# Two attention decodes on one core: the second half of every value chunk is copied to the spare buffer, and the last ten chunks load their keys in pieces

## The chip, the core and the metric

The kernel runs on one core of a Trainium2 chip. The metric is the time of one launch on the device in microseconds (us); the median of several launches counts. The core has a matmul engine (PE), a vector engine (DVE), a scalar engine (ACT), a general engine (POOL, called Pool below) and a sequencer that here only issues transfers (SP). Sixteen DMA engines carry the transfers between the memory of the chip (DRAM) and the core's on-chip buffer.

## The reference: what is computed

There are two independent decode steps of attention (one new token for each of four sequences); their results stand side by side in the output. For each, with `x` of 4 x 512, 32 query heads of width 128, and bf16 data:

```python
q = x @ wq                                   # 4 x 32 heads x 128
scores = einsum("bhqd,bhkd->bhqk", q, k) * 128 ** -0.5
p = softmax(scores)
o = einsum("bhqk,bhkd->bhqd", p, v)
out = o.reshape(4, 4096) @ wo                # 4 x 512
```

Problem A has 8 key heads, each shared by four query heads, and uses only the last 2048 positions of its cache. Problem B has 32 key heads and all 8192 positions: its keys and values are 4 x 32 x 8192 x 128 each, 268 MB of keys and as many of values, and each number is used once. Nearly all of the 587 MB that the kernel reads is this.

## The kernel before, in words

**Chunks.** Problem A is done first, in 8 chunks. Problem B follows in 32 chunks, which I number b0 to b31; the code's number is 8 more (`NCA` is 8, `NC` is 40, so `NC - 1` is b31 and `NC - 10` is b22). A B chunk is one sequence and four heads: 256 tiles of 128 positions x 128 for the keys (8.39 MB) and 256 tiles for the values (8.39 MB).

**Buffers.** `kv` has ten units; each holds 64 tiles. Units 0 to 3 (`KB`) take a B chunk's keys, units 4 to 7 (`VB`) its values, units 8 and 9 (`KX`) are the spare buffer. PE reads the first half of the keys in `KB`, and the second half in `KX`. For most chunks the keys come in one DMA into units 0 to 3, and Pool then copies the second half to `KX` in four copies of 32 tiles (L396), so that units 2 and 3 come free early. b0 and b27 to b31 are different: their keys come in pieces, and the pieces of the second half go straight to `KX`, with no copy. The values come in one DMA (in pieces for b27 to b31) and are read where they land.

**What a B chunk does (`whole_B`).** PE transposes each key tile into PSUM (L448, the groups "tr"), eight to a group; DVE (L517) or ACT (L515) copies a group to the buffer `kt`; PE multiplies it with the query (L450, "sc"). The 32 groups of a chunk run in order, with the score of a group two groups behind its transpose. Then come the maximum, the exponentials (ACT, L635), the sums (DVE, L640), with a reordering of the output weights beside them (PE L450 "tr<-wos", DVE L751). Then PE multiplies all 256 value tiles (L450, "po<-pbb,kv"), and the result is normalized (L725); its product with the output weights ("fin") is done in the next chunk. PE does all this in one fixed order, with no work of another chunk in between.

**What orders the transfers.** All of them are issued by SP from one list in program order: K(b0), V(b0), K(b1), V(b1) and so on, with the output weights `wos` behind the keys of every fourth chunk. SP stands still at an issue until the buffer is free, and all that follows on the list stands behind it. The list `held` says what frees a unit. A whole K(n+1) waits for the transposes of the first half of chunk n (units 0 and 1) and for the copies of the second half (units 2 and 3). V(n+1) waits for the last product of chunk n's values (key `("pv", c)`), for all four units (L412, issue at L415). The copies into `KX` wait for the transposes of the chunk before.

**How PE hears of a landing.** Pool stands between: for each landing it raises a counter (`relay`, a wait and an increment), `r_k` for the first half of the keys, `r_c` for the second (there the copy itself raises it), `r_v` for the values. Pool, too, works through one list in order. PE waits for steps of these counters: `QK` and `QC` for groups of key tiles, `QV` for the values.

Of the kernel before, what the change touches and what calls it, by code (L numbers as in the profile page):

```python
# [11 lines left out]
I32 = mybir.dt.int32  # L12

P = 128
TG = 8
NTRB = 3
NKT = 4
NH = 10
# [2 lines left out]
NSM = 2  # L21
SLAG = 2
NW = 64
LASTK = (32, 32, 64, 64, 64)
HALVES = (128, 128)
NEXTK = (64, 64, 64, 64)
NEXTV = (128, 64, 32, 32)
LASTV = (128, 64, 32, 16, 8, 8)
QK = (0, 4, 8)
QC = (16, 20, 24, 28)  # L30
QV = (0, 16, 24, 28, 30, 31)

TRM0, BC0, L0, Q0, XT0 = 0, 256, 288, 320, 448
Z0 = Q0
# [137 lines left out]
def bass_concat_heads__sliding_block_cached__mha_block_cached__decode_kernel(  # L172
# [23 lines left out]
    chunks = []  # L196
# [5 lines left out]
    NC = len(chunks)  # L202
    NCA = Hkv
# [8 lines left out]
    NTA, NTB = chunks[0]["NT"], chunks[-1]["NT"]  # L212
    NONE = NC
    chunks.append(dict(chunks[NCA]))
    assert sum(LASTV) == sum(LASTK) == sum(NEXTK) == sum(NEXTV) == NTB and NTA * 16 == 1024 and NTB * 4 == 1024

    sch = _Sched()
    with ExitStack() as es:
        block = es.enter_context(nc.Block())

        def sb(name, shape, dt):
            return es.enter_context(nc.sbuf_tensor(name, shape, dt))

        def ps(name, shape, dt):
# [4 lines left out]
        wos = sb("wos", [P, 4, DO], BF16)  # L229
# [36 lines left out]
        fin = ps("fin", [P, 512], F32)  # L266
        xtps = ms[:, XT0:XT0 + KC * NB].bitcast(BF16)

        semnames = ["eng_pe", "eng_dve", "eng_act", "eng_pool", "eng_sp", "d_x0", "d_x1", "d_o0", "d_o1", "r_k", "r_v"]
        semnames += ["d_h%d" % i for i in range(NH)] + ["d_bk0", "d_bv0", "r_c"]  # L270
        semnames += [f + str(i) for f, x in (("d_lk", LASTK), ("d_nk", NEXTK), ("d_fk", HALVES), ("d_lv", LASTV), ("d_nv", NEXTV), ("d_hv", HALVES)) for i in range(len(x))]
        semnames += ["d_wo%d" % i for i in range(NWO)] + ["d_wos"]
        sems = {n: es.enter_context(nc.semaphore(n)) for n in semnames}
# [15 lines left out]
            waits=["c_onesf", "c_identf"], key="c_ind")  # L289
# [26 lines left out]
        half_of = {}  # L316
        held = [[] for _ in range(NH)]
# [10 lines left out]
        def flat(at, n):  # L328
            return kv[:, at:at + n, :].rearrange("p s x -> p (s x)")
# [21 lines left out]
        def dma_wos(hq):  # L351


            src = B_wo[4 * hq * P:4 * (hq + 1) * P, :].rearrange("(p r) n -> p (r n)", r=4)
            sch.add_dma("sp", lambda e: e.dma_start(wos[:, :, :].rearrange("p r n -> p (r n)"), src), "d_wos",
                        waits=[("reord", NCA + 4 * hq - 1)] if hq else [], key=("wos", hq))

        def dma_A(kind, c):
# [4 lines left out]
            src = T[:, ch["g"], SkA - W:, :].rearrange("b (pp j) d -> pp b (j d)", pp=P // NB)  # L363
            sch.add_dma("sp", lambda e: e.dma_start(kv[:, at, :], src), "d_h%d" % at, waits=waits, key=(kind, c))

        def dma_K(c):


            ch, i0, half = chunks[c], c - NCA, NTB // 2
            src = B_k[ch["b"], 4 * ch["hq"]:4 * ch["hq"] + 4].rearrange("u (pp j) d -> (u pp) (j d)", pp=P // 4)  # L370
            T = [("T", ch["s"] + (u + 1) * NTB // 4 // TG - 1) for u in range(4)]
            wos = [("wos", ch["hq"])] if ch["b"] == 0 else []
            if c in PIECES_K:
                fam, pieces = PIECES_K[c]
                j0 = 0
                for i, n in enumerate(pieces):
                    at = KB if j0 < half else KX
                    dst = flat(at, 2)[:, (j0 % half) * P:(j0 % half + n) * P]
                    waits = []
                    for u in range(j0 % half * 4 // NTB, (j0 % half + n - 1) * 4 // NTB + 1):  # L380
                        waits += held[at + u]
                    x = slice(j0 * P, (j0 + n) * P)
                    sch.add_dma("sp", lambda e, x=x, dst=dst: e.dma_start(dst, src[:, x]), fam + str(i), waits=waits, key=("k", c, i))
                    j0 += n
                    if wos and j0 == NTB:
                        dma_wos(ch["hq"])
                    sch.relay("pool", sems, "r_k" if j0 <= half else "r_c", n // TG, [("k", c, i)] + (wos if j0 == NTB else []))
            else:
                sch.add_dma("sp", lambda e: e.dma_start(flat(KB, 4), src), "d_bk0", waits=held[KB] + held[KB + 1] + held[KB + 2] + held[KB + 3], key=("k", c, 0))
                if wos:  # L390
                    dma_wos(ch["hq"])
                sch.relay("pool", sems, "r_k", half // TG, [("k", c, 0)])
                for k in range(4):
                    x = slice(k * half // 4 * P, (k + 1) * half // 4 * P)
                    sch.ops["pool"].append((
                        lambda e, x=x: e.tensor_copy(flat(KX, 2)[:, x].bitcast(I32), flat(KB + 2, 2)[:, x].bitcast(I32)),  # L396
                        tuple(held[KX + k // 2] + [("k", c, 0)] + (wos if k == 3 else [])), ("r_c", half // 4 // TG), None))
                held[KB + 2] = held[KB + 3] = [("cp", c)]
                sch.tk[("cp", c)] = ("r_c", (i0 + 1) * half // TG)
            held[KB], held[KB + 1], held[KX], held[KX + 1] = [T[0]], [T[1]], [T[2]], [T[3]]  # L400
            for steps, name in ((QK, "r_k"), (QC, "r_c")):
                for g, end in zip(steps, steps[1:] + (steps[0] + half // TG,)):
                    sch.tk[("kr", c, g)] = (name, i0 * half // TG + end - steps[0])

        def dma_V(c):

            ch = chunks[c]
            src = B_v[ch["b"], 4 * ch["hq"]:4 * ch["hq"] + 4].rearrange("u (pp j) d -> (u pp) (j d)", pp=P // 4)
            dst = flat(VB, 4)
            fam, pieces = PIECES_V.get(c, ("d_bv", (NTB,)))  # L410
            j0 = 0
            waits = held[VB] + held[VB + 1] + held[VB + 2] + held[VB + 3]  # L412
            for i, n in enumerate(pieces):
                x = slice(j0 * P, (j0 + n) * P)
                sch.add_dma("sp", lambda e, x=x: e.dma_start(dst[:, x], src[:, x]), fam + str(i), waits=waits, key=("v", c, i))  # L415
                j0 += n
                sch.relay("pool", sems, "r_v", n // TG, [("v", c, i)])
            for g, end in zip(QV, QV[1:] + (NTB // TG,)):
                sch.tk[("vr", c, g)] = ("r_v", (c - NCA) * (NTB // TG) + end)
            for u in range(4):  # L420
                held[VB + u] = [("pv", c)]

        KB, VB, KX = 0, 4, 8
        PIECES_K = {NCA: ("d_fk", HALVES), NC - 5: ("d_fk", HALVES), NC - 4: ("d_fk", HALVES),
                    NC - 3: ("d_nk", NEXTK), NC - 2: ("d_nk", NEXTK), NC - 1: ("d_lk", LASTK)}
        PIECES_V = {NC - 5: ("d_hv", HALVES), NC - 4: ("d_hv", HALVES), NC - 3: ("d_nv", NEXTV), NC - 2: ("d_nv", NEXTV), NC - 1: ("d_lv", LASTV)}

        dma_x(0)
        dma_x(1)
# [16 lines left out]
        def pe_mm(o, l, r, start=True, stop=True, transpose=False, waits=(), key=None):  # L446
            if transpose:
                sch.add("pe", lambda e: e.transpose(o, l, r), waits, key)  # L448
            else:
                sch.add("pe", lambda e: e.matmul(o, l, r, start=start, stop=stop), waits, key)  # L450
# [35 lines left out]


        def tile_of(kind, c, j):
            if c >= NCA and kind == "k":
                return flat(KB if j < NTB // 2 else KX, 2)[:, j % (NTB // 2) * P:(j % (NTB // 2) + 1) * P]  # L490
            at = half_of[(kind, c)] if c < NCA else VB
            return flat(at, chunks[c]["NT"] // NTA)[:, j * P:(j + 1) * P]

        bank_used = [None] * NTRB

# [181 lines left out]
        def emit_pv(c, g):  # L677
            ch = chunks[c]
            UC = ch["UC"]
            base = 16 * (c % NSM) if ch["ab"] == 0 else 0  # L680
            for t in range(TG):
                j = g * TG + t
                n = NW
                waits = [("exp", c) if c < NCA else ("exp", c, 0)] + po_read if j == 0 else []
                if j == 0:
                    po_read[:] = []
                for k in (1, 2):
                    if c >= NCA and j == EXPS[k][0] - NW // 4:
                        waits = [("exp", c, k)]
                if c >= NCA:  # L690
                    waits += [("vr", c, g)] if t == 0 and g in QV else []
                elif j == 0:
                    waits += [("v", c)]
                pe_mm(po[:, base:base + n], tile_of("v", c, j), pbt[ch["ab"]][:, par(c), j * UC:j * UC + n],
                      start=j == 0, stop=j == ch["NT"] - 1, waits=waits, key=("pv", c) if j == ch["NT"] - 1 else None)

        def norm_sum(c):
            if c < NCA:
# [254 lines left out]
```

## Time and profile before

| what | value |
|---|---|
| median of three runs | 1381.54 us (1378.66 to 1383.99) |
| the profiled execution, its own time | 1391.14 us |
| its span, first to last instruction | 1389.4 us |
| busy PE, DVE, ACT, POOL | 90%, 54%, 39%, 15% of the span |
| read from DRAM | 587.21 MB, 423 GB/s over the span |
| granted PE clock, mean | 0.966 |
| one copy of keys by Pool (L396), 104 of them | 1.898 us |
| one copy of transposed keys, DVE (L517) / ACT (L515) | 0.691 us / 1.024 us |

The profile is of one execution, whose own time is 9.6 us above the median of the runs without a profile. [...] "DMA to landing" is the time from the issue of a transfer to its completion, and includes waiting behind the transfers before it.

### The profile page before, as it was taken

What the parts mean: (1) busy time and instruction counts of PE and PEld (TensorE: products, weight loads), DVE (VectorE), ACT (ScalarE), POOL (GpSimd) and SP (SyncE); (2) the same over time, 40 slices, a digit from 0 to 9 for tenths busy, and PEclk for the clock granted to TensorE, in tenths of its full rate; (3) what the DMA queues carried; (4) which work ended last, traced back from release to release, by engine and by line L of the source; (5) the groups of instructions that cost most, each with busy time, mean ns of one, the idle gap of its engine ahead of it and who ended that gap; (6) DMA issues with size and microseconds to landing.
All of it is one profiled execution on the core that took longest, in us unless ns stands there. A gap on an engine that the chain in (4) does not pass through costs nothing.

```text
span 1389.4 us, 61669 instructions
## 1 busy us (share of the span) xinstructions
PE 1244.8 (90%) x27673; PEld 1116.6 (80%) x27673; DVE 747.0 (54%) x1335; ACT 547.3 (39%) x777; POOL 202.5 (15%) x133
## 2 busy tenths in 40 slices
PE   4897898989899898989999899898998989999998
PEld 4776787878789787878888888787888878888887
DVE  1675364645455554545555555455655545556555
ACT  1553342434344333434444334343442433444443
POOL 2000022222101222220122222210222222000000
PEclk9998799999999999999999999999999999999999
DMA  9999899999999999999999999999999999999998
GB/s 399 426 425 443 382 423 423 419 425 426 434 394 451 411 419 425 392 438 423 426 449 419 423 441 413 432 438 423 434 411 453 432 428 419 423 428 428 427 428 360
DMA packets 17917, 587.52 MB, mean 423 GB/s; under 512 B 2004, under 2 KB 2024, under 8 KB 4456
## 3 DMA queue, kind: packets, MB, share of 16 engines
q1 hardware_dynamic: 17864, 587.21, 98.7%
q8 instruction: 15, 0.25, 0.1%
q14 instruction: 6, 0.05, 0.0%
q10 hardware_dynamic: 32, 0.01, 0.0%
HBM read 587.21 MB, written 0.01 MB: 423 GB/s over the span
## 4 chain that ended last, share of the span: by engine, by line
DMA 56%; PE 41%; DVE 1%; issue 1%; SPq 0%; POOLq 0%; DVEq 0%
DMA kv<-in_B_k_cache_dram 52%; PE tr L448 22%; PE sc L450 10%; PE po L450 5%; DMA kv<-in_A_k_cache_dram 2%; DMA kv<-in_B_wq_dram 2%; PE fin L450 2%; PE tr L450 1%; PE ms L450 1%; DVE kt L517 0%; DVE wor L751 0%; DVE sA L570 0%; DVE gm L601 0%; PE ms L448 0%; DVE rm L582 0%
## 5 line engine op out<-in xcount | busy, mean ns | idle before, releaser
L448 PE MATMUL tr<-identb,kv 128*128 128x128 bf16 x8704 | 679.9, 223 | 93.6 <-POOLq L75 85.0
L517 DVE COPY kt<-tr 128x1024 bf16<-128x1024 bf16 x736 | 502.7, 691 | 321.5 <-PE tr L448 318.7
L515 ACT ACTIVATE kt<-tr 128x1024 bf16<-128x1024 bf16 x352 | 359.6, 1024 | 693.9 <-PE tr L448 693.7
L448 PEld LDWEIGHTS tr<-identb,kv 128*128 128x128 bf16 x8704 | 520.2, 100 | 108.9 <-issue 87.1
L450 PE MATMUL sc<-qq,kt 128*128 128x64 bf16 x8192 | 402.0, 192 | 13.8 <-DVE kt L517 10.4
L450 PEld LDWEIGHTS sc<-qq,kt 128*128 128x128 bf16 x8192 | 335.7, 99 | 17.5 <-DVE kt L517 13.1
L396 POOL COPY kv<-kv 128x2048 int32<-128x2048 int32 x104 | 192.7, 1898 | 972.0 <-DMA kv<-in_B_k_cache_dram 972.0
L450 PEld LDWEIGHTS po<-pbb,kv 128*128 128x128 bf16 x8192 | 252.1, 99 | 10.7 <-issue 3.0
L450 PE MATMUL po<-pbb,kv 128*128 128x64 bf16 x8192 | 253.7, 194 | 2.4 <-issue 2.4
L635 ACT ACTIVATE pbb<-sc,negb 32x64 bf16<-32x64 f32 (+1 forms) x384 | 171.1, 445 | 131.5 <-DVE negb L615 126.3
L640 DVE TENSOR_REDUCE rsb<-pbb 128x4 f32<-128x1024 bf16 x32 | 39.1, 1220 | 99.8 <-ACT pbb L635 99.8
L751 DVE CAST wor<-tr 128x512 bf16<-128x512 f32 x128 | 80.1, 684 | 1.2 <-PE tr L450 1.2
L450 PE MATMUL po<-sel,identb 128*128 128x512 bf16 x256 | 77.2, 390 | 0.0
L450 PE MATMUL tr<-wos,back 32*128 32x512 bf16 x512 | 68.6, 384 | 3.1
L450 PEld LDWEIGHTS po<-sel,identb 128*128 128x128 bf16 x256 | 19.9, 98 | 39.6 <-issue 28.8
L586 DVE TENSOR_REDUCE rh<-sc 128x4 f32<-128x512 f32 x64 | 43.9, 686 | 14.3 <-PE sc L450 14.3
L450 PEld LDWEIGHTS tr<-wos,back 32*128 32x128 bf16 x512 | 21.7, 94 | 34.5 <-DVE wor L751 19.2
L725 DVE TENSOR_TENSOR oz<-po,rz 128x16 bf16<-128x16 f32 x32 | 5.6, 175 | 70.1 <-PE po L450 70.1
L450 PE MATMUL sc<-qb,kt 128*128 128x64 bf16 (+3 forms) x512 | 26.0, 196 | 0.7 <-DVE gx L607 0.6
L450 PE MATMUL fin<-wor,oz 128*4 128x256 bf16 x264 | 25.1, 324 | 0.4 <-DVE oz L725 0.4
L703 DVE RECIPROCAL rinv<-ms 128x4 f32<-128x4 f32 (+1 forms) x40 | 7.8, 196 | 30.6 <-PE ms L450 30.6
L450 PEld LDWEIGHTS sc<-qb,kt 128*128 128x128 bf16 x512 | 21.6, 101 | 2.7 <-DVE gx L607 1.1
(66 smaller groups left out, 252.2 us busy)
## 6 DMA issues: line engine op xcount, KB each, us to landing
kv<-in_B_v_cache_dram SPq DMA_DIRECT2D x7, 4096.0 KB, 23.1
kv<-in_B_k_cache_dram SPq DMA_DIRECT2D x6, 4096.0 KB, 21.6
kv<-in_B_k_cache_dram SPq DMA_DIRECT2D x11, 2048.0 KB, 30.4
kv<-in_A_k_cache_dram SPq DMA_DIRECT2D x8, 2048.0 KB, 14.6
kv<-in_A_v_cache_dram SPq DMA_DIRECT2D x8, 2048.0 KB, 16.1
kv<-in_B_v_cache_dram SPq DMA_DIRECT2D x3, 2048.0 KB, 30.4
kv<-in_B_v_cache_dram SPq DMA_DIRECT2D x5, 1024.0 KB, 32.4
kv<-in_A_wq_dram SPq DMA_DIRECT2D x1, 4096.0 KB, 12.5
```

The lines of the kernel that those rows point to most:

```text
L396: lambda e, x=x: e.tensor_copy(flat(KX, 2)[:, x].bitcast(I32), flat(KB + 2, 2)[:, x].bitcast(I32)),
L448: sch.add("pe", lambda e: e.transpose(o, l, r), waits, key)
L450: sch.add("pe", lambda e: e.matmul(o, l, r, start=start, stop=stop), waits, key)
L515: sch.add("act", lambda e: e.activation(dst, src, ACTF.Copy), waits=waits, key=("ev", s))
L517: sch.add("dve", lambda e: e.tensor_copy(dst, src), waits=waits, key=("ev", s))
L586: sch.add("dve", lambda e: e.tensor_reduce(out=rh[:, half, :], in_=src, axis=AX.X, op=ALU.max), waits=[("S", ch["s"] + (half + 1) * ch["NG ...
L635: sch.add("act", lambda e, src=src, dst=dst, pp=pp, u=u: e.activation(dst, src, ACTF.Exp, bias=negb[pp, 0, u:u + 1], scale=scale), waits=[ ...
L640: sch.add("dve", lambda e: e.tensor_reduce(out=rst[1][:, :], in_=probs_of(c).rearrange("p j u -> p u j"), axis=AX.X, op=ALU.add), waits=[( ...
L703: sch.add("dve", lambda e: e.reciprocal(out=ri, in_=ms[:, L0:L0 + n]), waits=[("L", c)], key=("rinv", c))
L725: sch.add("dve", lambda e: e.tensor_tensor(out=o, in0=i0, in1=i1, op=ALU.mult), waits=waits, key=("oT", c))
L751: sch.add("dve", lambda e: e.tensor_copy(wol[:, u, :], o), waits=[("reord", c) if u == 3 else ("reord", c, u)] + [("fin", prev(c))], key=( ...
```

## The change

Five things change.

1. Pool copies the second half of the values (units 6 and 7) to `KX` too, with the same four copies, as soon as the values have landed and the chunk's transposes have left `KX`. PE reads that half of the values from `KX`. A new counter `r_w` tells it so. This is done for b0 to b30.
2. V(n+1) now waits for the product of the first half of chunk n's values (units 4 and 5; a new signal in the middle of the product) and for the copies of the second half (units 6 and 7). `KX` now comes free for the keys of chunk n+1 with the product: three quarters of it for unit 8, all of it for unit 9.
3. The keys of b22 to b26 come in halves and those of b27 to b30 in quarters (before: b27 and b28 in halves, b29 and b30 in quarters, the others of these whole). Their second half lands in units 2 and 3 and is copied by Pool, and so is that of b31, whose second half now comes in four pieces in place of two. Only b0's keys still go straight to `KX`.
4. The values of b27 come whole (before: in halves). Those of b28 to b31 keep their pieces.
5. The second half of b31's values lands straight in `KX`, and waits for the transposes of b31's third and fourth quarter.

```diff
-LASTK = (32, 32, 64, 64, 64)
+LASTK = (32, 32, 64, 32, 32, 32, 32)
-QV = (0, 16, 24, 28, 30, 31)
+QV = (16, 20, 24, 28, 30, 31)
...
+        def spread_copies(name, units, waits, first, n, landed, last=()):
+            for k in range(first // 32, (first + n) // 32):
+                x = slice(k * 32 * P, (k + 1) * 32 * P)
+                sch.ops["pool"].append((
+                    lambda e, x=x: e.tensor_copy(flat(KX, 2)[:, x].bitcast(I32), flat(units, 2)[:, x].bitcast(I32)),
+                    tuple(waits[k // 2] + landed + (list(last) if k == 3 else [])), (name, 32 // TG), None))
...
 dma_K:
+            direct = c == NCA
+            units = [KB, KB + 1] + ([KX, KX + 1] if direct else [KB + 2, KB + 3])
...
+                    if direct:
+                        sch.relay("pool", sems, "r_c", (j0 + n - half - first) // TG, [key] + end)
+                    else:
+                        spread_copies("r_c", KB + 2, [held[KX], held[KX + 1]], first, j0 + n - half - first, [key], end)
...
 dma_V:
-            waits = held[VB] + held[VB + 1] + held[VB + 2] + held[VB + 3]
+            direct = c == NC - 1
+            units = [VB, VB + 1] + ([KX, KX + 1] if direct else [VB + 2, VB + 3])
...
+                    else:
+                        spread_copies("r_w", VB + 2, [held[KX], held[KX + 1]], first, j0 + n - half - first, [key])
...
-            for u in range(4):
-                held[VB + u] = [("pv", c)]
+            if not direct:
+                held[VB + 2] = held[VB + 3] = [("cw", c)]
+                sch.tk[("cw", c)] = ("r_w", (i0 + 1) * half // TG)
+            held[VB] = held[VB + 1] = [("pv", c, 2)]
+            held[KX], held[KX + 1] = [("pv", c, 3)], [("pv", c)]
...
-        PIECES_K = {NCA: ("d_fk", HALVES), NC - 5: ("d_fk", HALVES), NC - 4: ("d_fk", HALVES),
-                    NC - 3: ("d_nk", NEXTK), NC - 2: ("d_nk", NEXTK), NC - 1: ("d_lk", LASTK)}
-        PIECES_V = {NC - 5: ("d_hv", HALVES), NC - 4: ("d_hv", HALVES), NC - 3: ("d_nv", NEXTV), NC - 2: ("d_nv", NEXTV), NC - 1: ("d_lv", LASTV)}
+        PIECES_K = {NCA: ("d_fk", HALVES), NC - 1: ("d_lk", LASTK)}
+        PIECES_K.update({c: ("d_fk", HALVES) for c in range(NC - 10, NC - 5)})
+        PIECES_K.update({c: ("d_nk", NEXTK) for c in range(NC - 5, NC - 1)})
+        PIECES_V = {NC - 4: ("d_hv", HALVES), NC - 3: ("d_nv", NEXTV), NC - 2: ("d_nv", NEXTV), NC - 1: ("d_lv", LASTV)}
...
 emit_pv (c is the chunk, j its value tile, NTB is 256):
-                      start=j == 0, stop=j == ch["NT"] - 1, waits=waits, key=("pv", c) if j == ch["NT"] - 1 else None)
+                      start=j == 0, stop=j == ch["NT"] - 1, waits=waits,
+                      key=("pv", c) if j == ch["NT"] - 1 else ("pv", c, (j + 1) // 64) if c >= NCA and j in (NTB // 2 - 1, NTB // 4 * 3 - 1) else None)
```

PE, DVE and ACT do the same work in the same order as before; only PE's waits and signals around the value products differ. Pool has 248 copies in place of 104, and SP has a few more issues.

More of the change, by code (lines that the diff above doesn't have):

```diff
@@ L267, in bass_concat_heads__sliding_block_cached__mha_block_cached__decode_kernel @@
         xtps = ms[:, XT0:XT0 + KC * NB].bitcast(BF16)
-        semnames = ["eng_pe", "eng_dve", "eng_act", "eng_pool", "eng_sp", "d_x0", "d_x1", "d_o0", "d_o1", "r_k", "r_v"]
+        semnames = ["eng_pe", "eng_dve", "eng_act", "eng_pool", "eng_sp", "d_x0", "d_x1", "d_o0", "d_o1", "r_k", "r_v", "r_w"]
         semnames += ["d_h%d" % i for i in range(NH)] + ["d_bk0", "d_bv0", "r_c"]
@@ L372, in dma_K @@
             wos = [("wos", ch["hq"])] if ch["b"] == 0 else []
[L373 to L397, printed above, removed]
@@ new lines, in dma_K @@
+            direct = c == NCA
+            fam, pieces = PIECES_K.get(c, ("d_bk", (NTB,)))
+            units = [KB, KB + 1] + ([KX, KX + 1] if direct else [KB + 2, KB + 3])
+            landed, j0 = [], 0
+            for i, n in enumerate(pieces):
+                at = units[j0 // 64]
+                waits = []
+                for u in range(j0 // 64, (j0 + n - 1) // 64 + 1):
+                    waits += held[units[u]]
+                x, y = slice(j0 * P, (j0 + n) * P), slice(j0 % 64 * P, (j0 % 64 + n) * P)
+                sch.add_dma("sp", lambda e, x=x, y=y, at=at: e.dma_start(flat(at, NH - at)[:, y], src[:, x]), fam + str(i), waits=waits, key=("k", c, i))
+                landed.append((j0, n, ("k", c, i)))
+                j0 += n
@@ new lines, in dma_K @@
+            if wos:
+                dma_wos(ch["hq"])
+            for j0, n, key in landed:
+                end = wos if j0 + n == NTB else []
+                if j0 < half:
+                    sch.relay("pool", sems, "r_k", min(n, half - j0) // TG, [key])
+                if j0 + n > half:
+                    first = max(j0, half) - half
+                    if direct:
+                        sch.relay("pool", sems, "r_c", (j0 + n - half - first) // TG, [key] + end)
+                    else:
+                        spread_copies("r_c", KB + 2, [held[KX], held[KX + 1]], first, j0 + n - half - first, [key], end)
@@ L405, in dma_V @@
         def dma_V(c):
-            ch = chunks[c]
+            ch, i0, half = chunks[c], c - NCA, NTB // 2
             src = B_v[ch["b"], 4 * ch["hq"]:4 * ch["hq"] + 4].rearrange("u (pp j) d -> (u pp) (j d)", pp=P // 4)
-            dst = flat(VB, 4)
             fam, pieces = PIECES_V.get(c, ("d_bv", (NTB,)))
+            direct = c == NC - 1
+            units = [VB, VB + 1] + ([KX, KX + 1] if direct else [VB + 2, VB + 3])
             j0 = 0
-            waits = held[VB] + held[VB + 1] + held[VB + 2] + held[VB + 3]
@@ L413, in dma_V @@
             for i, n in enumerate(pieces):
-                x = slice(j0 * P, (j0 + n) * P)
-                sch.add_dma("sp", lambda e, x=x: e.dma_start(dst[:, x], src[:, x]), fam + str(i), waits=waits, key=("v", c, i))
-                j0 += n
-                sch.relay("pool", sems, "r_v", n // TG, [("v", c, i)])
+                at = units[j0 // 64]
+                waits = []
+                for u in range(j0 // 64, (j0 + n - 1) // 64 + 1):
+                    waits += held[units[u]]
+                x, y = slice(j0 * P, (j0 + n) * P), slice(j0 % 64 * P, (j0 % 64 + n) * P)
@@ new lines, in dma_V @@
+                sch.add_dma("sp", lambda e, x=x, y=y, at=at: e.dma_start(flat(at, NH - at)[:, y], src[:, x]), fam + str(i), waits=waits, key=("v", c, i))
+                key = ("v", c, i)
+                if j0 < half:
+                    sch.relay("pool", sems, "r_v", min(n, half - j0) // TG, [key])
+                if j0 + n > half:
+                    first = max(j0, half) - half
+                    if direct:
+                        sch.relay("pool", sems, "r_w", (j0 + n - half - first) // TG, [key])
+                    else:
+                        spread_copies("r_w", VB + 2, [held[KX], held[KX + 1]], first, j0 + n - half - first, [key])
@@ L418, in dma_V @@
+                j0 += n
+            if not direct:
+                held[VB + 2] = held[VB + 3] = [("cw", c)]
+                sch.tk[("cw", c)] = ("r_w", (i0 + 1) * half // TG)
+            held[VB] = held[VB + 1] = [("pv", c, 2)]
+            held[KX], held[KX + 1] = [("pv", c, 3)], [("pv", c)]
+            sch.tk[("vr", c, 0)] = ("r_v", (i0 + 1) * half // TG)
             for g, end in zip(QV, QV[1:] + (NTB // TG,)):
-                sch.tk[("vr", c, g)] = ("r_v", (c - NCA) * (NTB // TG) + end)
@@ L420, in dma_V @@
-            for u in range(4):
-                held[VB + u] = [("pv", c)]
+                sch.tk[("vr", c, g)] = ("r_w", i0 * half // TG + end - QV[0])
         KB, VB, KX = 0, 4, 8
-        PIECES_K = {NCA: ("d_fk", HALVES), NC - 5: ("d_fk", HALVES), NC - 4: ("d_fk", HALVES),
-                    NC - 3: ("d_nk", NEXTK), NC - 2: ("d_nk", NEXTK), NC - 1: ("d_lk", LASTK)}
-        PIECES_V = {NC - 5: ("d_hv", HALVES), NC - 4: ("d_hv", HALVES), NC - 3: ("d_nv", NEXTV), NC - 2: ("d_nv", NEXTV), NC - 1: ("d_lv", LASTV)}
+        PIECES_K = {NCA: ("d_fk", HALVES), NC - 1: ("d_lk", LASTK)}
@@ L488, in tile_of @@
         def tile_of(kind, c, j):
[L489 to L492, printed above, removed]
+            if c >= NCA:
+                return flat(KX if j >= NTB // 2 else KB if kind == "k" else VB, 2)[:, j % (NTB // 2) * P:(j % (NTB // 2) + 1) * P]
+            return flat(half_of[(kind, c)], 1)[:, j * P:(j + 1) * P]
         bank_used = [None] * NTRB
@@ L690, in emit_pv @@
                 if c >= NCA:
-                    waits += [("vr", c, g)] if t == 0 and g in QV else []
+                    waits += [("vr", c, g)] if t == 0 and (g == 0 or g in QV) else []
                 elif j == 0:
```

## The prediction

> **What bounds the kernel now.** I read the page first.
>
> ```profile
> PE 1244.8 (90%) x27673; PEld 1116.6 (80%) x27673; DVE 747.0 (54%) x1335; ACT 547.3 (39%) x777; POOL 202.5 (15%) x133
> q1 hardware_dynamic: 17864, 587.21, 98.7%
> DMA kv<-in_B_k_cache_dram 52%; PE tr L448 22%; PE sc L450 10%; PE po L450 5%; DMA kv<-in_A_k_cache_dram 2%; DMA kv<-in_B_wq_dram 2%; PE fin L450 2%; PE tr L450 1%; PE ms L450 1%; DVE kt L517 0%; DVE wor L751 0%; DVE sA L570 0%; DVE gm L601 0%; PE ms L448 0%; DVE rm L582 0%
> ```
>
> PE at 90% and the transfers at 98.7% both look full; the chain of waits says that it is mostly the keys' transfer that ends a wait. So the second view is the chain in order of time, in the steady part:
>
> ```profile
> 984.69 25.98 DMA kv<-in_B_k_cache_dram
> 1010.84 1.06 PE tr L448 x16
> ...
> 1021.87 28.58 DMA kv<-in_B_k_cache_dram
> 1050.62 1.37 PE tr L448 x16
> ...
> 1063.17 26.02 DMA kv<-in_B_k_cache_dram
> 1089.36 1.06 PE tr L448 x16
> ```
>
> Start plus length is the landing of a chunk's keys: 1010.67, 1050.45, 1089.19. PE starts 0.17 us after each, so PE waits for every chunk. The spacings are 39.78 and 38.74, and 38.72 is the shortest that I find (two transfers of 19.36). Why is one longer by 1.04? The third view, SP's issues:
>
> ```profile
> 1009.22 0.33 SPq L415 DMA_DIRECT2D kv<-in_B_v_cache_dram  x1
> 1021.87 0.33 SPq L389 DMA_DIRECT2D kv<-in_B_k_cache_dram  x1
> 1046.39 0.33 SPq L415 DMA_DIRECT2D kv<-in_B_v_cache_dram  x1
> ```
>
> The values of b22 were issued at 1009.22, 1.4 us before the keys ahead of them in the queue had landed; those of b23 at 1046.39, 4.1 us before. Only the first cost time. Over all chunks a lead of 3 us or more costs nothing, 2.15 us (issue at 333.29, keys landed 335.44) costs 1.7, and a negative lead up to 3.4. The view by stretches shows the queue running dry there (last columns: DMA share and GB/s; before them, Pool's busy time and the clock):
>
> ```profile
> 250.00:260.00 10.00, 9.09 (x236) 8.44 (x233) 5.37 (x9) 1.66 (x2) 5.52 (x4) 1.00 0.79 315
> 570.00:580.00 10.00, 9.09 (x250) 8.58 (x247) 4.08 (x9) 1.71 (x3) 3.69 (x3) 1.00 0.77 308
> 1090.00:1100.00 10.00, 10.00 (x229) 9.63 (x227) 6.78 (x10) 4.38 (x5) 6.83 (x4) 1.00 0.98 426
> ```
>
> What holds V back is in SP's waits:
>
> ```profile
> SPq L415 <- PE po L450: 623.1, 32, 40.2
> ```
>
> V(n+1) waits for the last value product of chunk n, which ends 35.5 us after the keys of n landed (1010.84 to 1046.39), or 37.1 where PE had idled before and its clock was granted at 0.83 for a while (1050.62 to 1087.69). The queue ahead of it is empty at 38.7. The lead of 1.6 to 3.2 us is too short.
>
> **What the gaps are worth.** Keys of b1 landed at 173.5 (issue 133.8 and 39.7 to landing), those of b26 at 1168.5: 995.0 us for 25 spacings. At 38.72 they are 968.0; six loads of `wos` lie between, 1.27 each: 7.6. The excess is 19.4 us. V(b26) was late too (issue 1166.42, 1.0 lost): 20.4. Of this, 1.4 stands at chunks whose V was in time; I leave it, and 19.0 remains.
>
> **The change part by part.**
>
> V's wait: the second half of the product takes 3.95 us (256 tiles in 7.9), so the first half ends at 31.6 (slow chunks 33.1) after the keys' landing. The other condition, Pool's copies of V's second half: V lands at 19.4; units 8 and 9 are free after the third and fourth quarter of the transposes, at 16.3 and 21.8 (slow 17.8 and 23.3); a set of four copies takes 7.4 us. Two copies are done by 23.1, two more by 27.0. So V(n+1) is issued at 31.6 to 33.1, a lead of 5.6 to 7.1 us in place of 1.6 to 3.2; every lead over 3 was free. Gain 19.0. At b1, where most is lost (V issued at 174.4, keys landed at 173.5), the half product ended at 166.6 and the copies can be done at 161.8, so it holds there too. What is late next: nothing on PE, which needs 35.5 to 37.1 per chunk against 38.7; the transfers themselves are the bound until the last chunk.
>
> Pool: 144 more copies of 1.9 us, 273 us; Pool goes from 15% to about 34%. Queued behind V's copies on Pool are the relay and copies of the next keys. V's copies are done at 27.0, the next keys land at 38.7: nobody waits. The next keys' copies now also wait for the end of the product (35.5 to 37.1), again before 38.7. Cost 0; with the cover gone, one copy (1.9) a chunk.
>
> A rule of the Trainium skill speaks against this part: "SBUF — State Buffer", section "Who interferes with whom", says that a DVE copy or cast in a two-port mode and a Pool instruction exclude each other for a whole instruction, and that DMA never contends with an engine. First the rows: eight L517 copies beside Pool's copies (1090 to 1097) average 690 ns, eight without Pool (1245 to 1252) 692; the four Pool copies beside them take 7.41 us in every chunk. By the row, V's copies cost DVE nothing; by the rule, if these DVE operations took the shared port, four copies would hold PE's feeders up to 7.4 us a chunk. I take 0: L517 reads PSUM, as do the casts L751 that two of the new copies will lie beside. The sum L640 reads the on-chip buffer, and no row shows it beside Pool; a block of 1.9 there would still leave PE under 38.7 (35.5 + 1.9). Below zero there is nothing: no operation is removed. That transfers do not suffer from Pool has a row too: keys of b23 landed 1050.45, values 1069.81 (issue 1046.39 and 23.4), 19.36 with four copies beside them, the shortest there is.
>
> Pieces of keys: a transfer in quarters took 19.57 in place of 19.36 (b30), in halves 19.4, in eighths 0.14 more for half a chunk. Two more chunks in quarters, three more in halves, b31's second half finer, V of b27 no longer split: about +0.6 in all, on the path. What they bring: PE starts 10 to 15 us before a chunk's keys are complete, and need not wait in b22 to b30. That is not on the path once the queue never runs dry; 0. In b27 PE will instead wait for V, which comes whole (0 on the path, V is early enough for its successors), and in b28 to b30 a copy of 1.9 us serves 1.0 us of product, so the product ends 1 to 2 us after V's last landing.
>
> **The end.** It is the last view, the chain from b31's third piece of keys on:
>
> ```profile
> 1323.13 32.94 DMA kv<-in_B_k_cache_dram
> 1356.16 0.62 PE tr L448 x8
> ...
> 1377.57 5.72 PE po L450 x171
> ```
>
> From that landing (1356.07) PE runs without a stall to 1389.4: 33.3 us. The piece is 64 tiles in both kernels. Before it, PE is at tile 64 of b31; in the changed kernel b30's product ends about 1 us later against the transfers, tile 64 at 9.2 after the start of K(b31)'s transfer (1346.2, 9.9 before 1356.07), the piece at 9.9: still hidden. Tiles 128 to 255 now wait for Pool: landings 2.5 apart (12.3, 14.8, 17.2, 19.7), copied 1.9 later; PE wants them at 15.3, 18.0, 20.7 and 23.4. Hidden by 1.1 or more; the whole cost if not is 1.9. The second half of V(b31) waits for transposes that end at 20.7 and 26.1; the queue is empty at 29.5. Hidden. So the tail of 33.3 stays.
>
> Sum: span 1389.4 - 19.0 + 0.6 = 1371.0, own time 1391.1 - 18.4 = 1372.7.
>
> **From there to the median.** The profiled execution is 9.6 us above the median. If that is spread evenly, the median falls by as much as the profiled time: 1381.5 - 18.4 = 1363.1. If the transfers run at the same pace without a profile and the 9.6 are all gaps, the change takes them from both, and the median ends where the profile does: 1372.7. No row tells which; I take the middle, 1368.
>
> **Rivals.**
>
> (a) Part of the gain is not there in timed runs, or comes back: gaps of only 9 us to begin with (1381.5 - 1372.7 + 0.6 = 9.4), and Pool's extra copies slow transfers by 1% over their 273 us (2.7), or the end loses a copy or two (1.9 to 3.8). 1381.5 - 9.4 + 0.6 + 3.8 = 1376.5. For it: the 9.6 us; against it: leads so short that they cost time in 10 of the 26 chunks b1 to b26, of which a run without a profile would have to avoid half.
>
> (b) Slower: the shared port. If V's copies and DVE do exclude each other, PE's chunk grows from 35.5 by up to 7.4 to 42.9 and passes 38.7; PE is then the bound, and 30 chunks x 4.2 = 126 us less the 18.4: about 1489. It decides from 3.2 us lost a chunk on, and makes the kernel slower by 0.5% from 4.1. The 690 against 692 ns speak against it.
>
> (c) The change does not do what it says: V's issue moves to the end of Pool's copies instead, because V lands late or Pool is late. It needs copies at 35.5, 8.5 us later than computed; then 1381.5 + 0.6 = 1382.
>
> **Chances.** Likeliest case 0.70 (1362 to 1374), (a) 0.18 (1374.6 to 1380), (c) 0.06, (b) 0.06. A measurement of this kernel tells 0.5% (6.9 us) from no change, so faster means under 1374.6: 0.70 and a little of (a), 0.73; within 0.5%: 0.21; slower 0.06. The range takes in the likeliest case and most of (a): 1361 to 1378.
>
> **What would show it.** Right: no stretch with a DMA share under 0.9 between 120 us and the end; keys' landings 38.7 apart; V issued 5 to 7 us before the keys ahead have landed; L517 still near 691 ns with 248 copies on Pool; last landing of values near 1367. Wrong: SP's value issue waiting for Pool instead of PE; longer Pool copies; packets slower beside them; PE waiting for Pool in b31.

## The result, and the profile after

The changed kernel takes 1373.65 us (median of four runs, 1372.11 to 1374.75) beside 1381.33 for the kernel before: a ratio of 0.9944 with a 95% interval of 0.9921 to 0.9966. In a later comparison it was 1372.93 beside 1383.51 (0.9924, 0.9899 to 0.9949). The profiled execution took 1372.73 us, with a span of 1371.0. So it is faster by 8 to 11 us, less than the 13.5 us that I took as likeliest, and its profiled execution is where the sum had it. Ratios and their intervals, here and below, are estimated over all executions and are not quotients of the medians.

The page of the changed kernel, with the lines that answer to those of before:

```profile
PE 1243.0 (91%) x27640; PEld 1115.7 (81%) x27673; DVE 767.7 (56%) x1335; ACT 546.9 (40%) x777; POOL 469.6 (34%) x277
q1 hardware_dynamic: 19304, 587.21, 99.6%
```

The share of the transfers is up from 98.7% to 99.6%, and no slice of the span (34 us each) is below 0.9 before the last. DVE is busy for 20.7 us more, with the same 1335 instructions: that is new, and I come back to it. The chain in order of time, in the steady part of the changed kernel:

```profile
653.30 27.51 DMA kv<-in_B_k_cache_dram
...
693.56 25.96 DMA kv<-in_B_k_cache_dram
...
730.72 27.53 DMA kv<-in_B_k_cache_dram
```

The landings are 680.81, 719.52 and 758.25, so 38.71 and 38.73 apart, and not 39.78 and 38.74 in turn. From the keys of b1 (173.26) to the last half of b26's (1150.17) it is 976.9 us for 25 spacings, where 968.0 and 7.6 for the output weights are the least: an excess of 1.3, which was 19.4. SP's issues say why:

```profile
206.57 0.33 SPq L429 DMA_DIRECT2D kv<-in_B_v_cache_dram  x1
223.17 0.33 SPq L392 DMA_DIRECT2D kv<-in_B_k_cache_dram  x1
244.68 0.33 SPq L429 DMA_DIRECT2D kv<-in_B_v_cache_dram  x1
261.88 0.33 SPq L392 DMA_DIRECT2D kv<-in_B_k_cache_dram  x1
283.37 0.33 SPq L429 DMA_DIRECT2D kv<-in_B_v_cache_dram  x1
```

The keys ahead of these three landed at 211.98, 250.68 and 289.38: leads of 5.4, 6.0 and 6.0 us. Over b2 to b21 the lead is 3.0 to 7.8. SP's waits, first one line of the kernel before, then three of the changed kernel (a wait at L106 can be for a V or for a K):

```profile
SPq L106 <- POOL kv L396: 256.7, 25, 13.1
...
SPq L106 <- POOL kv L372: 607.0, 42, 28.0
SPq L392 <- PE sc L477: 228.3, 36, 15.8
SPq L429 <- PE po L477: 189.1, 29, 16.5
```

Of V's 623 us of waiting for the product (L415 before), 189 are left. The wait for Pool's copies was there before for the keys alone; some 350 us have come to it, and they are V's. It ends before the product's half does: at 206.57 V is issued 0.03 us after the last product of that half (206.54).

### The profile page after: what moved, and what is told of

Read it like the earlier page. It is cut to its first block, busy times and chain, and to the rows that moved or that the text cites. A ratio compares the mean times of both kernels' runs of the same rounds, so it can differ in the third digit from the quotient of the medians.

```text
span 1371.0 us, 61779 instructions
## 1 busy us (share of the span) xinstructions
PE 1243.0 (91%) x27640; PEld 1115.7 (81%) x27673; DVE 767.7 (56%) x1335; ACT 546.9 (40%) x777; POOL 469.6 (34%) x277
## 3 DMA queue, kind: packets, MB, share of 16 engines
q1 hardware_dynamic: 19304, 587.21, 99.6%
## 4 chain that ended last, share of the span: by engine, by line
DMA 55%; PE 38%; DVE 3%; issue 1%; POOL 1%; ACT 0%; SPq 0%; POOLq 0%; DVEq 0%
DMA kv<-in_B_k_cache_dram 43%; PE tr L475 20%; DMA kv<-in_B_v_cache_dram 9%; PE sc L477 9%; PE po L477 5%; DMA kv<-in_B_wq_dram 2%; PE fin L477 2%; POOL kv L372 1%; DMA kv<-in_A_k_cache_dram 1%; PE ms L477 1%; PE tr L477 1%; DVE sA L596 1%; DVE rm L615 0%; DVE kt L543 0%; DVE wor L778 0%
## 5 line engine op out<-in xcount | busy, mean ns | idle before, releaser
L372 POOL COPY kv<-kv 128x2048 int32<-128x2048 int32 x248 | 459.8, 1894 | 878.4 <-DMA kv<-in_B_k_cache_dram 299.7
L475 PE MATMUL tr<-identb,kv 128*128 128x128 bf16 x8704 | 670.6, 222 | 47.2 <-POOLq L75 39.6
L475 PEld LDWEIGHTS tr<-identb,kv 128*128 128x128 bf16 x8704 | 512.4, 99 | 60.4 <-issue 38.2
L477 PEld LDWEIGHTS po<-pbb,kv 128*128 128x128 bf16 x8192 | 260.6, 100 | 22.5 <-issue 11.6
L477 PE MATMUL po<-pbb,kv 128*128 128x64 bf16 x8192 | 262.7, 196 | 10.8 <-POOL kv L372 4.4
L666 DVE TENSOR_REDUCE rsb<-pbb 128x4 f32<-128x1024 bf16 x32 | 39.0, 1220 | 95.9 <-ACT pbb L661 95.9
L477 PE MATMUL tr<-wos,back 32*128 32x512 bf16 x512 | 71.8, 391 | 3.0
L477 PE MATMUL po<-sel,identb 128*128 128x512 bf16 x224 | 71.3, 415 | 0.0
L477 PEld LDWEIGHTS tr<-wos,back 32*128 32x128 bf16 x512 | 22.0, 94 | 35.5 <-DVE wor L778 19.4
L475 PE MATMUL ms<-identf,rm 128*4 128x128 f32 x40 | 11.1, 278 | 24.4 <-DVE rm L615 20.6
L615 DVE TENSOR_TENSOR rm<-rh 128x4 f32<-128x4 f32 x32 | 23.7, 740 | 1.1
```

The lines of the kernel that those rows point to most:

```text
L615: sch.add("dve", lambda e: e.tensor_tensor(out=rm[:, m, :], in0=rh[:, 0, :], in1=rh[:, 1, :], op=ALU.max), waits=[("rh", c, 1)], key=("row ...
L666: sch.add("dve", lambda e: e.tensor_reduce(out=rst[1][:, :], in_=probs_of(c).rearrange("p j u -> p u j"), axis=AX.X, op=ALU.add), waits=[( ...
```

## A cost that the prediction did not have

Where did DVE's 20.7 us come from? Most of it is the tile `rm`, the maximum over a chunk's scores that precedes the exponentials. Before, at L589 (duration least / median / most, in ns):

```profile
L589 DVE TENSOR_TENSOR rm<-rh x32: 161/162/165, 154.6 to 1374.3; 128x4 f32<-128x4 f32 x32
```

and in the changed kernel, where the same line is L615:

```profile
L615 DVE TENSOR_TENSOR rm<-rh x32: 161/544/1853, 151.7 to 1355.8; 128x4 f32<-128x4 f32 x32
```

Its 32 executions now sum to 23.7 us and were 5.2, which is 18.5 of the 20.7. (A second operation with two inputs, `rz`, has 4.5 us more, and `qq`, a small copy, 1.5 less; both come up below.) Its longest is about the length of one of Pool's copies (1.89). The timeline of the changed kernel at b11 shows Pool, then DVE, then PE:

```profile
582.98 7.40 POOL L372 COPY kv<-kv 128x2048 int32<-128x2048 int32 x4 [12.53 <-PE tr L475]
```

```profile
586.72 1.84 DVE L615 TENSOR_TENSOR rm<-rh 128x4 f32<-128x4 f32 x1
588.92 0.28 DVE L627 TENSOR_REDUCE gm<-ms 4x4 f32<-4x128 f32 x1 [0.36 <-PE ms L475]
```

```profile
588.62 0.27 PE L475 MATMUL ms<-identf,rm 128*4 128x128 f32 x1 [1.67 <-DVE rm L615]
593.56 6.67 PE L477 MATMUL po<-pbb,kv 128*128 128x64 bf16 x168
```

Pool's four copies follow each other every 1.84 us, so the third starts at 586.65. The maximum starts 0.07 us later and ends with it, at 588.56; PE stands for 1.67. How long the maximum is held depends on where it falls in a copy: at b3 it starts 0.64 us into the third copy and takes 1257 ns, and nine of the 32 lie between 1254 and 1269. At b11 the values landed 0.6 us later, and Pool's copies with them. And PE then pays a second time, as its clock goes down. The view by stretches (the clock is the third number from the end):

```profile
584.00:588.00 4.00, 2.64 (x55) 1.93 (x53) 3.34 (x4) 0.52 (x1) 4.00 (x3) 1.00 0.98 426
588.00:592.00 4.00, 3.14 (x11) 1.02 (x11) 2.79 (x6) 2.05 (x6) 2.38 (x2) 0.78 0.98 426
592.00:596.00 4.00, 4.00 (x50) 2.87 (x50) 1.32 (x2) 3.25 (x7) 0.00 (x0) 0.50 1.02 442
596.00:600.00 4.00, 4.00 (x125) 4.00 (x123) 0.59 (x1) 0.00 (x0) 0.00 (x0) 0.87 0.81 347
```

The clock is at 0.50 for the whole of the third stretch and for parts of its neighbours (0.78 and 0.87), 6.8 us in all. The first 168 value products take 6.67 us, where the kernel before has this line for b11:

```profile
603.87 5.12 PE L450 MATMUL po<-pbb,kv 128*128 128x64 bf16 x168
```

So b11 needs 40.0 us on PE from its first transpose to its last product, against 35.5: 1.7 of standing and 2.8 at the lower clock.

Is the lower clock due to the blocked maximum? I count over b1 to b23 the chunks whose clock falls to 0.50 between the maximum and the last product. There are 7 in the changed kernel, 5 in its second profile (experiment 6) and 9 in experiment 3, all behind a maximum of 1.1 us or more. There is none in the kernel before, none in experiment 4, and none in experiments 6 and 7 with a maximum that Pool does not block. A block does not always bring it: 16 others of 1.1 us or more in those three profiles (b3 above is one) are followed by none.

Five of the 31 chunks after b0 need 39 us or more, longer than the transfers' 38.7: b11, b20 and b23 in this way, b27 and b28 because they wait for values. The transfers hardly show it: V(b12) still had a lead of 3.0 us over the keys of b12, and a load of the output weights lies between the two.

## The experiments

Theory V says that V's wait for the end of the product starves the queue of transfers, and that its earlier issue is the whole gain. Theory L says that Pool's copies block the maximum of two operands and so make PE's chunks long. The rivals stand in the expectations.

**1. The kernel before, again.** No edit.

> The kernel before, unchanged, for a second profile beside more timed runs. Theory G (the profiled execution of before lay 9.6 us above the median because of its gaps): a profile near 1381 us shows 25 spacings of key landings that exceed 38.72 us plus the output weights by about 9 to 10 us in all, not 19.4, with V issued late in fewer chunks or less late. Rival S (an execution is slower as a whole, transfers too): the excess is again near 19 us and single packets or spacings are shorter than 38.7. Time by both: 1381, ratio 1.000.

Measured: 1385.38 beside 1383.16, ratio 1.0004 (0.9982 to 1.0027); 64 executions of the same program lie between 1379.6 and 1395.4. The profiled one took 1387.1. Its excess over 25 spacings is 15.6 us (keys of b1 at 173.3, of b26 at 1164.5), where the first profile had 19.4: 3.8 less in excess, 4.0 less in time. Theory G holds in its mechanism; my number for it did not, as this profile was again of a long execution. The 9.6 us are no offset of the profiler's: the changed kernel's profiled execution (1372.73) lies below its median. The kernel before has a wide spread, and between these two executions the gaps are nearly all of it; for the executions without a profile that is not shown.

**2. The pieces of keys alone.** In the kernel before, only the keys' part is new (`dma_K`, `PIECES_K`, `LASTK`):

```diff
-LASTK = (32, 32, 64, 64, 64)
+LASTK = (32, 32, 64, 32, 32, 32, 32)
...
+        PIECES_K.update({c: ("d_fk", HALVES) for c in range(NC - 10, NC - 5)})
+        PIECES_K.update({c: ("d_nk", NEXTK) for c in range(NC - 5, NC - 1)})
```

> The kernel before with the new pieces of keys alone (b22 to b26 in halves, b27 to b30 in quarters, their second halves copied by Pool); the values are loaded and waited for as before. Theory V (V's wait for the end of the product starves the queue, and nothing else does): only the gaps of b22 to b26 go, 0 to 2 us in before, and the pieces cost 0.6, so 1380 to 1382, ratio 0.999 to 1.001. Rival K (the pieces of keys bring the gain, as PE gets ahead in the last ten chunks): 1373 to 1376, ratio under 0.997.

Measured: 1382.12 beside 1383.16, ratio 0.9990 (0.9976 to 1.0003). Theory V; rival K is out.

**3. The value copies alone.** In the changed kernel, `LASTK`, `PIECES_K` and `PIECES_V` are those of before.

> The changed kernel with the old sizes of the pieces of keys (b0, b27, b28 halves, b29, b30 quarters, b31 32, 32, 64, 64, 64) and V of b27 in halves; value copies and the earlier wait as in the changed kernel. Theory V: 1373, equal to the changed kernel within 1 us, ratio 0.994. Rival K: 1378 to 1381.

Measured: 1377.64 beside 1383.16, ratio 0.9948 (0.9931 to 0.9965); 1373.2 to 1382.5. Between the two expectations, and 4 to 5 us over the changed kernel (1373.65 and 1372.93). Neither theory as I had it: the copies bring the gain, but not all of it reaches the end. In its profile the maximum has a median of 898 ns, and eight chunks of b6 to b24 take 39 us or more.

**4. Values in halves, no copies.** In the kernel before, every V in two transfers, each with its own wait:

```diff
-            fam, pieces = PIECES_V.get(c, ("d_bv", (NTB,)))
+            fam, pieces = PIECES_V.get(c, ("d_hv", HALVES))
...
+                waits = held[VB] + held[VB + 1] if j0 < NTB // 2 else held[VB + 2] + held[VB + 3]
...
-                held[VB + u] = [("pv", c)]
+                held[VB + u] = [("pv", c, 2)] if u < 2 else [("pv", c)]
```

> The kernel before, with every chunk's values in two halves: the first half waits for the product of the first half of the values of the chunk before, the second for the end of that product. No copy of values by Pool, and the spare buffer serves the keys alone. Theory V: the lead of the first half is what counts; its 9.7 us of transfer cover the 4 us until the product ends, so there are no gaps, and halves cost 0.05 us for each of 27 chunks, 1.4 in all: 1374 to 1375, ratio 0.995. If the copies do something more than bring V's issue forward (rival C: V's whole 19.4 us must stand in the queue), gaps stay, and it is 1378 to 1381.

Measured: 1372.37 beside 1383.16, ratio 0.9914 (0.9881 to 0.9947), and all six runs between 1372.29 and 1372.54. Theory V, with no help from Pool at all; the time is some 2 us below what I expected. Leads of V's first half are 5.1 to 8.3 over b2 to b26, and the excess over the 25 spacings is 1.5. The tile `rm` here:

```profile
L589 DVE TENSOR_TENSOR rm<-rh x32: 161/162/165, 152.1 to 1355.4; 128x4 f32<-128x4 f32 x32
```

Copies that only make room for an earlier issue are not needed, if the transfer is cut where the room comes free.

**5. The copies, but the late wait.** In the changed kernel one line:

```diff
-            held[VB] = held[VB + 1] = [("pv", c, 2)]
+            held[VB] = held[VB + 1] = [("pv", c)]
```

> The changed kernel with one wait put back: the first half of the next values waits for the end of the value product again, not for its first half. Copies, pieces and counters stay. Theory V (the earlier wait is what pays): the gaps are back, and since PE's chunks are longer than before by the blocked maximum, leads are shorter still: 1383 to 1388, ratio 1.000 to 1.004, key landings 39 to 40.5 apart. Rival (the freed buffer or the pieces pay, whatever the wait): below 1377.

Measured: 1395.27 beside 1383.76, ratio 1.0065 (1.0041 to 1.0088), from 1381 to 1401 in 19 executions and 1409 in one. Theory V, and worse than expected. Its profile is of a short execution (1386.6 span): leads of V down to -0.5 us, and b9 to b11 at 41.5, 40.5 and 39.8 us on PE. The copies without the earlier wait are a loss.

**6. The changed kernel again, and the maximum by a reduce.** These two and experiments 7 and 8 have the same runs of the kernel before beside them (1383.51). The first has no edit; the second is the changed kernel with

```diff
-                sch.add("dve", lambda e: e.tensor_tensor(out=rm[:, m, :], in0=rh[:, 0, :], in1=rh[:, 1, :], op=ALU.max),
+                sch.add("dve", lambda e: e.tensor_reduce(out=rm[:, m, :], in_=rh[:, :, :].rearrange("p h u -> p u h"), axis=AX.X, op=ALU.max),
```

> The changed kernel, unchanged, beside the next two. Theory L (Pool's copy holds the port that a DVE operation with two inputs in the on-chip buffer needs: the small maximum rm at L615 grows from 0.16 us to up to one copy, PE idles in the softmax, its clock is halved for some us, and a chunk grows from 35.5 to up to 40 us): 1373 to 1376, with a spread of 2 us or more between runs, and some chunks of 38.7 us and more. Rival D (the changed kernel is at the floor of the transfers already, L costs nothing on the path): 1372.5 with a spread under 1 us, as the kernel with values in halves had.

> The changed kernel with one DVE operation written otherwise: the maximum of the two half maxima is a reduce over one operand (rh, 4 x 2) in place of an operation of two operands. Same values, copies and waits. Theory L: the operation takes 0.1 to 0.2 us in all 32 chunks though Pool copies beside it, PE's chunks are 35.5 to 37.1, time 1372 to 1373 with a spread under 1 us. Rival: if it is the copies' traffic or their order on Pool that holds DVE and not the second operand, the reduce is as long as the maximum was (up to 1.9) and the time stays with the changed kernel.

Measured: the changed kernel 1372.93 (1371.67 to 1375.76), with the reduce 1371.30 (1370.71 to 1371.91), ratio to before 0.9909 (0.9885 to 0.9933). Five of the changed kernel's six executions are longer than all six with the reduce. The operation is back to its length, though Pool copies as much as before. The first line is of all chunks, the others of b11:

```profile
L615 DVE TENSOR_REDUCE rm<-rh x32: 160/161/164, 154.2 to 1355.0; 128x4 f32<-128x8 f32 x32
...
582.68 7.41 POOL L372 COPY kv<-kv 128x2048 int32<-128x2048 int32 x4 [11.95 <-PE sc L477]
586.98 0.16 DVE L615 TENSOR_REDUCE rm<-rh 128x4 f32<-128x8 f32 x1
592.00:596.00 4.00, 4.00 (x137) 3.99 (x134) 1.22 (x1) 2.09 (x4) 0.00 (x0) 1.00 0.95 410
```

The clock stays at 1.00, and b11 takes 35.5 us. So it is the maximum's form, two operands in the on-chip buffer, that lets Pool block it. The edit changes the kind of instruction too, but `rz`, which keeps its two operands in the on-chip buffer, is still blocked in this run, in six of the chunks b24 to b30:

```profile
L735 DVE TENSOR_TENSOR rz<-rinv,pm x32: 174/176/1830, 163.9 to 1364.5; 128x16 f32<-128x16 f32 x32
```

PE's chunks go up to 38.2 until b23, without those of 39 and 40. Theory L; what it costs the changed kernel at the end is only 1.6 us, and the spread. This version is the fastest of all, by a hair.

**7. The value copies alone, with the reduce.** Experiment 3 with the edit of 6.

> The kernel with the value copies alone (old pieces of keys), which had 1377.6, with the same rewritten maximum. Theory L: its 4 to 5 us over the floor come from chunks made long by the blocked maximum, with PE late at the end and no pieces of keys to catch up on; so 1372 to 1374. Rival K2 (the pieces of keys are needed for the gain whatever DVE does): 1376 to 1378 as before.

Measured: 1372.66 (1371.69 to 1376.33), ratio 0.9924 (0.9898 to 0.9949). That is 5.0 us below experiment 3 by the medians, and 3.3 by the ratios, whose intervals overlap; five of the six executions are at 1373.2 or below, and one of experiment 3's 21. So the blocked maximum is what cost experiment 3 most of its 4 to 5 us. It is still 1.4 over the version with the finer keys, and the chain of its end says where (the first line is the third piece of b31's keys, landed at 1336.1):

```profile
1303.18 32.94 DMA kv<-in_B_k_cache_dram
1336.22 0.62 PE tr L474 x8
...
1341.16 1.90 POOL kv L372
1343.11 0.62 PE tr L474 x8
```

A fourth piece of 64 tiles lands at 1341.0, Pool copies its first half, and PE stands until 1343.1. From the third piece to the end it is 34.8 us, and 33.4 in the changed kernel, whose pieces of 32 land in time to be copied.

**8. Copies of 16 tiles.** In `spread_copies` of the changed kernel, 32 becomes 16, with the waits and the counter's steps to match, so that 496 copies run.

> The changed kernel with each of Pool's copies cut in two (16 tiles each, 496 copies). Theory L (exclusive for the length of one instruction): a copy takes about 1.0 us and the longest rm 0.16 plus one copy, at most 1.1 us in place of 1.85; median near 0.3 to 0.6. Rival (DVE gets a share of the port): the longest stays near 1.85. One look: 1372 to 1374.

Measured: a single execution, 1371.57 us, which alone says little of the time. A copy takes 1.04 us, and the maximum

```profile
L615 DVE TENSOR_TENSOR rm<-rh x32: 161/267/1005, 154.1 to 1354.7; 128x4 f32<-128x4 f32 x32
```

has a longest of 1.0 and a median of 0.27: it waits for one instruction of Pool's at most, 1.04 or 1.89 us long, and does not share. In b1 to b23 the clock falls behind none of these shorter blocks.

**9. Value copies twice.** In the changed kernel Pool makes each value copy twice, and the second raises the counter.

> The changed kernel with each of Pool's value copies done twice, one after the other, the second raising the counter: 124 more copies, 235 us more on Pool. By my prediction's costing (Pool has room, DVE does not feel it) V is still issued with a lead of 4 us or more and the time stays at 1373. Theory L: Pool now copies through the whole stretch in which the maximum of two operands falls, so rm is blocked in nearly every chunk (median over 0.8 us), many of PE's chunks are 38 to 41 us, about the transfers' 38.7, and the time is 1378 to 1400.

Measured: 1397.91 beside 1382.45, ratio 1.0109 (1.0084 to 1.0135). Inside the range of theory L, but hardly by its mechanism. The maximum has a median of 708 ns, not over 800:

```profile
L618 DVE TENSOR_TENSOR rm<-rh x32: 163/708/1851, 154.3 to 1380.3; 128x4 f32<-128x4 f32 x32
```

In all it takes 25.4 us, and 23.7 in the changed kernel, so it is blocked little more than there. What is new is plain lateness of Pool. Its eight copies take 15.5 us, and V waits for their end: its lead is 3.6 in most chunks. In b3 to b26, where no output weights stand between, V's transfers take 0.1 to 1.5 us more than 19.35, 0.7 in the mean. In b22 to b28 the second half of the product takes 6 to 8 us instead of 4, as it waits for copies; those chunks need 39 to 41 us. Of the 24.4 us that the profiled span is longer than that of the changed kernel, 13.5 are in the 25 spacings and 10.7 behind the keys of b26. What it shows is the margin: twice the copies turn a gain of 9 us into a loss of 15.

## Why the prediction was right, and where not

**What bounds the kernel, and the worth of the gaps: right.** 19.0 us were to go; the excess fell from 19.4 to 1.3, and behind the keys of b26 the span is as long as before (220.8 and 220.9 us). That the profiled span is 1371.0, the number of the sum, is in its last digits luck: the changed kernel's second profile has 1370.6. Experiments 4 and 5 show that it is V's wait: the earlier issue without copies has the whole gain, and the copies without the earlier issue have none.

**V's lead: right in kind, too good in size.** 5.6 to 7.1 us were computed, 3.0 to 7.8 measured; those under 5 follow a blocked maximum and a lower clock (3.0 after b11). The limit of 3 us, over which a lead was to cost nothing, is no sharp one: leads of 3.0 to 3.1 lost from nothing to 1.5 us in experiment 3, and those of 3.6 up to 1.3 in experiment 9. In the kernel before, 2.76 lost nothing at b17 and 2.8 us at b9.

**Pool's cost to DVE: wrong.** The step "By the row, V's copies cost DVE nothing" took L517's 690 against 692 ns for all of DVE. L517 is still at 691 in the changed kernel, with more than twice the copies, but the row is of an operation with one input, in PSUM. I went on to the sum L640 as the one case that no row shows (it took 1220 ns before and after), and did not list the maximum L589, which reads two inputs from the on-chip buffer. The rule of the Trainium skill has this half too ("SBUF — State Buffer", "Who interferes with whom": a DVE instruction with two inputs in that buffer contends with a Pool instruction that reads it, and the contention is an exclusive lock); I quoted the half on copies and casts, and here rule and measurement agree: 161 ns become up to 1853. The profile of before also had a row of a blocked copy with one input, within the on-chip buffer at the start of b3, and I did not look for it (which mode it ran in, no run shows):

```profile
L526 DVE COPY qq<-qs x32: 168/169/1625, 123.1 to 1348.3; 128x4 bf16 x32
254.77 1.62 DVE L526 COPY qq<-qs 128x4 bf16 x1 [0.51 <-issue]
254.48 7.42 POOL L396 COPY kv<-kv 128x2048 int32<-128x2048 int32 x4 [31.25 <-DMA kv<-in_B_k_cache_dram]
```

It ends at 256.40, 0.03 us after the first of the four copies. So it was already untrue of the kernel before that DVE feels nothing of Pool, and a second operand is not the only way into the block.

The stall was bounded at 1.9 us, and is that; what multiplied it is PE's clock, which made 1.7 us of standing into 4.5 at b11. It cost the changed kernel 1.6 us (experiment 6), because, I think, 3.2 us of slack a chunk cover most of it, and 3 to 5 us where PE has no finer keys to catch up with (3 against 7). The point of 3.2 us a chunk from which rival (b) was to decide is passed in single chunks only.

**Pieces of keys: the cost was right in size, "not on the path" was not.** They delay the transfers by the 0.6 us of the sum: the third piece of b31's keys lands at 1336.75 in the profile with the reduce (6) and at 1336.12 with the old pieces (7). But with the copies in place they bring 1.4 us net (7 against 6) where I had -0.6, since the tail is 33.4 us and not 34.8, and more where PE is late. By themselves they bring about nothing (experiment 2).

**The end: right.** The tail is 33.4 us from the third piece's landing (1337.61), predicted 33.3.

**From the profile to the median: the mis-sized term.** I took the middle of 1363.1 and 1372.7. The second was right: medians are 1373.65 and 1372.93. The profiled execution of before was a long one among executions from 1379 to 1395 (experiment 1), and its surplus over the second profile was nearly all gaps (3.8 of 4.0 us), which the change takes from every execution. That is rival (a)'s first term, gaps of 9 us to begin with. So the likeliest gain of 13.5 us was too large by the half of the 9.6 us that I had put into it.

## What to carry to other kernels

When a full queue of transfers shows a spacing that alternates, measure each issue's lead over the landing ahead of it: the gain of an earlier issue is the sum of what the short leads cost, and ends at the floor of the transfers. If the profiled execution lies above the median of a kernel that loses time to such gaps, take the floor as the forecast, not the difference. Before giving a second engine copies as "free" work, go through every small operation of the neighbour that it may block, by its number of inputs and by where they lie, and look in the profile for one whose longest is far over its median; then ask what an idle microsecond does to the next engine's clock. Here, cutting the transfer in two was simpler and as fast.

## What was not expected of the hardware

A maximum of 128 x 4 numbers on DVE takes 161 ns, and up to 1853 ns when it reads two operands while Pool copies 32 tiles, 1005 ns when Pool copies 16; as a reduce over one operand it takes 161 beside the same copies. A copy of 128 x 4 numbers took 1625 ns in place of 169 beside a copy of Pool's. After 1.7 us of waiting on PE in the softmax of b11, where PE is thinly used anyway, the granted clock was 0.50 for 6.8 us.
